# A state-space convolution and a gated MLP on one core: late groups rounded by ScalarE, seven absolute values on ScalarE, single PSUM banks for three stages, and another order

## The chip, the core and the metric

The kernel runs on one core of a Trainium2 chip. A core has five engines that run side by side, each through its own instructions in order: TensorE (PE, with its weight loads shown apart as PEld), VectorE (DVE), ScalarE (ACT), GpSimd (POOL) and SyncE (SP). SP, POOL and ACT also issue DMA transfers, each through its own queue. Products of TensorE land in PSUM, eight banks of 512 float32 values per partition; everything else is kept in SBUF, 128 partitions wide. The metric is the device time of one launch in microseconds.

## The reference

Two blocks on a sequence of 2048 rows and 576 channels, each behind a layer norm with a modulation that comes from a condition vector `c`:

```python
mod = (silu(c) @ w_mod).reshape(1, 6, 1, 576)         # sa, ca, ga, sb, cb, gb
h = layernorm(x) * (1 + ca) + sa
x = x + ga * A(h)                                      # state-space convolution
h = layernorm(x) * (1 + cb) + sb
x = x + gb * B(h)                                      # gated MLP

# A: K[d, l] = Re sum_n C[d,n] exp(dt[d] A[d,n] l) dt[d] B[d,n],  n < 128, l < 2048
#    y = causal convolution of h with K along l (by FFT) + h * Dskip
# B: z = gelu(x @ w_in); g = w_sp @ layernorm(z2) + b_sp; (z1 * g) @ w_out
```

What matters here is A. Its kernel K needs, for each channel and pole, an exponential of the real part and the sine and cosine of the imaginary part of `dt A l`.

## The kernel before, in words

The program has two parts. `ssm` does block A in the first quarter of the span; the class `Mlp` does block B in the rest. The change touches `ssm` only.

`ssm` computes the convolution by a hand-made transform of length 2048, split as 32 by 64. It is built of units, Python generators that issue a few instructions at each step. The units that matter:

- `O`, `P`: the poles. From the raw parameters, logarithms, phases and their three-part bf16 splits are computed on DVE and ACT and stored to DRAM (`pa_d`, `pb_d`, on POOL's queue); `Q` loads them back as `lb`, `lc`, `la` (POOL's queue), one set for nine groups.
- `M` (`mod_unit`): one of the six modulation vectors: a product over the partitions, a copy, a product with ones, and a last step that differs by vector. `M2`, `M1`, `M0` give what the first layer norm needs, `M0` in an alternation of ACT and DVE that splits its result in bf16 parts; `M3` to `M5` are for the MLP. `i` (POOL's queue) and `w` (SP's queue) load the weights.
- `S`, `R`, `A`: layer-norm statistics of four row blocks (`x` and `j` load them, two buffers), the rows themselves on DVE, and `ln_half`, the first transform: sixteen small products in two 288-column halves, four results of 288 columns each, copied by ACT to `st1o` and stored to `u1_d` in DRAM (POOL's queue).
- for each of 36 groups of 16 channels: `e` (an exponent product and two exponentials on ACT), `t` (a phase product, the rounding to the nearest turn, the absolute value, and two sines on ACT), `p` (products of these on DVE), `k` (64 small products into `kab`), `1` (`k1_unit`, the 32-point product, copied to the tile `k1`).
- `u`, `z`, `v`, `y`: for each of 36 slices the second transform of the rows (`u`, with a DMA that swaps real and imaginary halves, `uu` to `uu`), the product with the transformed kernel (`z`), the way back (`v`, stored to `v_d`), and the last transform with the residual (`y`, stored to `x1_d`). `U`, `W`, `X` load their inputs on SP's queue.

In `t_unit`, `ROUNDED` says how the phase is reduced to a fraction of a turn. For a group in the set (all 36 before), PE adds and takes away a large constant in PSUM: four products of 512 columns for the constant and eight of 256 for the phase, twelve in all, and the remainder is left in PSUM. DVE takes its absolute value by masking the sign bit into `ct`, ACT takes the sine of the remainder and the sine of the absolute value, shifted (a cosine). For a group outside the set, PE makes four products of 256 columns, ACT copies with the constant added, DVE subtracts both to get the remainder in SBUF, masks the sign bit there, and ACT takes both sines from SBUF.

PSUM is shared out in two pools: `ps2`, two buffers of two banks each, for `M`, `A`, the first product of `e`, `t` and `1`; and `ps1`, four buffers of one bank, for the second product of `e`, for `k`, `u`, `z`, `v`, `y`.

The sequence on every engine is written out by hand in the string `ORDER`: a word such as `t14` takes the next step of unit `t` for number 14, and each engine runs its instructions in just this order (`Pinned` keeps it). Capital letters without steps issue loads or change pools. `C0` closes the pools of the early units (`O`, `P`, `M`, `S`, `R`, `A`) and opens those of `u`, `z`, `v`, `y`; `D0` ends the tables' pools and starts the MLP's; the words `L0` to `L17` are the MLP's first loads and scalings. Line 182 in the profile is the helper that issues every pinned instruction, so groups are told apart by their tiles: `ps` and `pk` are the two PSUM pools, `et` exponentials, `ft` a group's phase and sines, `pg` the products of `p`, `kab` and `k` the results of `k` and `1`.

Of the kernel before, what the change touches and what calls it, by code (L numbers as in the profile page):

```python
# [12 lines left out]
I32 = mybir.dt.int32  # L13
# [16 lines left out]
ROUNDED = set(range(36))  # L30
COPIED = set()
ORDER = """
B2 i2 B0 B7 O0 O0 O0 O0 O0 O0 j1 O0 M2 O0 O0 i1 x0 O0 O0 O0 O0 B6 O0 B4 O0 M1 O0 O0 O0 B1 B3 O0 O0 S0 M2 O0 w3 O0 O0 O0 P0 O0 O0 B5 O0 O0 M2 P0 S1 S0 O0 g1 S0 P0 O0 P0 S1
S0 P0 P0 S0 Q0 P0 g0 P0 M2 S0 i0 e0 e0 t0 t0 M1 M1 M1 t2 P0 P0 t0 S1 e0 P0 t2 t2 P0 S1 t0 R0 P0 R2 M0 e2 M0 M0 e2 M0 e1 e5 e1 M0 e0 O0 R1 t1 e5 e4 M0 P0 t1 e1 t1 P0 t3 p0
p0 t1 P0 p0 M0 t3 t3 k0 M0 e3 t2 e5 e4 e1 M0 P0 k0 R3 10 P0 e3 e3 e2 10 S1 P0 A0 S1 A0 A0 A0 A1 e2 p2 P0 e3 A1 A1 A1 A0 A2 p1 r2 p1 p1 t3 p2 P0 A2 A1 P0 A2 k1 A2 A3 k1 A3
A3 R5 A3 p3 R4 t4 p2 r3 A2 t4 t4 11 11 e4 A4 R7 A3 P0 A4 k2 R6 A4 p3 j2 A4 A5 A5 O0 A5 A4 t4 P0 S2 A5 M3 k2 e4 M3 A6 S2 A6 A6 w4 A6 e6 P0 t5 e5 S2 e6 p4 S2 t5 M3 t5 M3 M4
a4 12 t5 S2 A5 M4 P0 M4 M3 p3 e6 p4 12 P0 P0 k3 M4 A7 A7 P0 e6 A7 A7 e8 P0 k3 O0 e7 e8 M4 t6 e7 13 A6 t6 O0 R9 w5 x3 R8 13 M5 t6 P0 M5 p4 t6 A8 S3 S3 A7 P0 A8 A8 A8 k4 S3
S3 A9 a5 Q1 A9 S3 A8 R10 A9 A9 r6 M5 R11 P0 k4 O0 R12 14 M5 e7 p6 14 p6 P0 O0 R13 P0 A10 A9 A10 e7 e8 p6 p5 O0 O0 A10 P0 A10 A11 p5 A11 A11 A11 r7 k6 A12 A10 p5 R14 A12
A12 k5 t7 A11 A12 t7 t7 A13 t7 P0 k5 k6 A13 R15 O0 A13 O0 p7 P0 t8 A13 t8 t8 15 p7 15 A12 t8 A14 p7 A14 A14 A14 A13 e8 P0 k7 p8 A15 A15 P0 k7 A14 A15 e10 A15 M5 e9 e10
A15 e9 C0 e11 e9 e10 p8 p8 e11 e9 t10 k8 t10 Q2 e11 t9 e10 U5 t10 t10 t9 p10 t9 U1 t11 U9 t11 t11 U2 U0 u1 u5 u1 t9 c2 16 16 17 p10 17 p10 u2 k8 U6 u5 t14 p9 u0 k10 t14  # L40
t11 u2 18 p9 t14 U10 z5 e14 k10 u5 18 e12 e11 u6 u1 p9 e14 z5 c0 u0 e12 e14 v5 110 u0 p11 e13 e12 p11 v5 k9 110 U7 p11 u6 e13 z1 e18 v5 c1 e15 e14 z1 U13 k11 e18 z0 t12
# [153 lines left out]
def ssm(tc, I, x1_d, consts_s, dram, mod_d, mlp):  # L195
# [3 lines left out]
    HC = 288  # L199
    CW = 16 * 9 * 128  # L200
    with ExitStack() as ctx:
# [1983 lines left out]
```

## Time and profile before

| what | value |
|---|---|
| median of 3 runs | 1782.7 us (1779.5 to 1788.4) |
| the profiled execution | 1781.2 us, span 1779.5 us |
| PE busy | 1665.9 us, 94% of the span |
| DVE busy | 1233.0 us, 69% |
| ACT busy | 828.9 us, 47% |
| POOL busy | 248.3 us, 14% |
| mean granted PE clock | 0.969 |
| table loads on ACT | 44, 1283 ns each |
| state-space part | from 0 to about 447 us |

Engine shares are averages over stages with different limits, so the stage is what must be looked at. Busy PE is not PE at its peak: the ends of matmuls are modelled, and a matmul that is pipelined behind another counts from its own start, so durations of neighbours overlap. A float32 product is issued as two instructions. What a unit of work costs an engine is therefore read from start to start, where the engine runs without a gap.

### The profile page before, as it was taken

Reading aid. Unit: us, or ns where it says so; the run is one execution under the profiler, and the core shown is the slowest. Engines: PE = TensorE matmul, PEld = TensorE weight load, DVE = VectorE, ACT = ScalarE, POOL = GpSimd, SP = SyncE. Lnnn points to the kernel's source line nnn. Section 1 sums busy time; section 2 is a strip of 40 time slices with the busy share of each in tenths; the row PEclk is TensorE's granted clock in tenths of the full one; section 3 lists DMA queues with packets and bytes.
Section 4 is the critical chain, followed back from the end, with each engine's and each line's share of the span. In section 5 each row is a group of like instructions: output and inputs, shape, how many; then the busy total and the mean of one; then the engine's idle time right before and its main releaser. Section 6 shows DMA issues by size and latency. Waiting matters only on the chain.

```text
span 1779.5 us, 38363 instructions
## 1 busy us (share of the span) xinstructions
PE 1665.9 (94%) x16246; PEld 1240.0 (70%) x16246; DVE 1233.0 (69%) x2173; ACT 828.9 (47%) x1117; POOL 248.3 (14%) x412
## 2 busy tenths in 40 slices
PE   2677899997899999999989999999999999999999
PEld 0334556565455545787878888888888888888887
DVE  5776787766999998788898768688344478344432
ACT  4867888863577666445434443234232223122210
POOL 3242232232222211000000000000111100111100
PEclk9577999999899999999999999999999999999999
DMA  8274667689688778777665886773766573556531
GB/s 245 63 241 155 182 185 209 175 217 276 202 273 275 242 226 278 285 250 245 224 210 174 298 291 224 270 245 124 245 223 229 196 234 99 193 196 218 193 111 41
DMA packets 182939, 376.42 MB, mean 212 GB/s; under 512 B 39104, under 2 KB 102976, under 8 KB 182000
## 3 DMA queue, kind: packets, MB, share of 16 engines
q1 hardware_dynamic: 138304, 168.56, 31.1%
q0 software_dynamic: 37984, 178.55, 30.4%
q10 hardware_dynamic: 6480, 26.86, 3.7%
q8 instruction: 127, 2.08, 0.5%
q14 instruction: 44, 0.36, 0.1%
HBM read 263.18 MB, written 101.31 MB: 205 GB/s over the span
## 4 chain that ended last, share of the span: by engine, by line
PE 67%; DVE 15%; DMA 5%; issue 4%; ACT 2%; POOL 1%; SPq 0%; ACTq 0%; DVEq 0%; POOLq 0%
PE ps L182 58%; PE pk L182 9%; DVE bsz L182 2%; DMA zset<-set_d 2%; DVE n L182 1%; DVE zset L182 1%; DVE rq L182 1%; DVE gt L182 1%; DVE wso L182 1%; DMA uu<-uu 1%; DVE wsp L182 1%; DVE nt L182 1%; DMA wsst<-in_w_spT 1%; DVE bsx L182 1%; DMA z_d<-z 1%
## 5 line engine op out<-in xcount | busy, mean ns | idle before, releaser
L182 PEld LDWEIGHTS <-zset 128*128 128x128 f16 x7182 | 701.3, 98 | 97.4 <-DVE zset L182 8.1
L182 PE MATMUL ps<-wsp,zset 128*128 128x256 f16 x6048 | 669.1, 273 | 9.9 <-DVE zset L182 6.3
L182 PE MATMUL pz<-wz,nt 128*128 128x512 f16 (+1 forms) x1120 | 223.6, 360 | 8.0 <-ACT nt L182 2.7
L182 ACT ACTIVATE z<-gt 128x1024 f16<-128x1024 f32 x56 | 59.0, 1054 | 282.0 <-DVE gt L182 281.9
L182 PEld LDWEIGHTS <-nt 128*128 128x128 f16 x1120 | 109.3, 99 | 116.3 <-issue 5.4
L1893 POOL DMA_DIRECT2D zset<-set_d x96 | 50.8, 529 | 872.9 <-PE ps L182 619.3
L182 DVE SCALAR_TENSOR_TENSOR gt<-ps,sc,bsp 128x512 f32<-128x512 f32 x36 | 27.0, 750 | 207.6 <-PE ps L182 205.9
L182 PE MATMUL ps<-wout,z 128*128 128x288 f16 x1344 | 170.1, 286 | 0.0
L182 PEld LDWEIGHTS <-z 128*128 128x128 f16 x1344 | 131.2, 98 | 33.3
L182 PE MATMUL ps<-n2o,zset 128*128 128x256 f16 x1134 | 128.2, 273 | 0.0
L182 DVE SCALAR_TENSOR_TENSOR gt<-ps,sc,gt 128x512 f32<-128x512 f32 (+1 forms) x180 | 122.2, 696 | 7.6
L182 DVE TENSOR_TENSOR raw<-raw 128x512 f32<-128x512 f32 (+2 forms) x228 | 119.1, 528 | 10.6 <-DMA raw<-z_d 6.3
L182 ACT ACTIVATE zset<-raw 128x1792 f16<-128x1792 f32 x48 | 81.2, 1692 | 61.4 <-PE ps L182 33.4
L182 DVE TENSOR_TENSOR zset<-raw,zset 128x1792 f16<-128x1792 f32 x48 | 97.0, 2020 | 17.2 <-ACT zset L182 17.2
L182 DVE TENSOR_TENSOR z<-ps,z 128x512 f32<-128x512 f32 (+1 forms) x126 | 71.9, 598 | 36.8 <-ACT z L182 26.7
L182 DVE TENSOR_TENSOR pg<-et,ft 128x1024 f32<-128x1024 f32 x72 | 85.9, 1218 | 11.9 <-ACT et L182 6.5
L182 DVE TENSOR_TENSOR zz<-pk,uu 128x1024 f32<-128x1024 f32 x36 | 43.9, 1222 | 39.0 <-PE pk L182 31.3
L182 PE MATMUL pk<-zz,small 128*128 128x512 f32 x144 | 69.4, 608 | 0.2 <-DVE zz L182 0.2
L182 ACT ACTIVATE wsp<-raw,sc 128x1792 f16<-128x1792 f32 x25 | 44.6, 1784 | 42.7 <-DVE raw L182 35.0
L182 ACT ACT_TABLE_LOAD x44 | 56.5, 1283 | 16.4 <-DMA et<-in_A_B_re 14.3
L182 DVE TENSOR_SCALAR ft<-ps 128x1024 int32<-128x1024 int32 x36 | 43.8, 1221 | 27.7 <-PE ps L182 26.8
L182 ACT ACTIVATE z<-z,sc 128x1024 f32<-128x1024 f32 x21 | 24.1, 1148 | 75.6 <-DVE z L182 71.9
(299 smaller groups left out, 2357.2 us busy)
## 6 DMA issues: line engine op xcount, KB each, us to landing
zset<-set_d POOLq DMA_DIRECT2D x96, 896.0 KB, 4.9
raw<-z_d SPq DMA_DIRECT2D x48, 512.0 KB, 5.5
set_d<-zset ACTq DMA_DIRECT2D x24, 896.0 KB, 6.0
z_d<-z POOLq DMA_DIRECT2D x32, 576.0 KB, 8.7
zset<-wa_d POOLq DMA_DIRECT2D x18, 896.0 KB, 4.9
raw<-in_w_spT SPq DMA_DIRECT2D x25, 512.0 KB, 4.5
set_d<-zset SPq DMA_DIRECT2D x12, 896.0 KB, 5.3
u_d<-st1o POOLq DMA_DIRECT2D x16, 576.0 KB, 4.6
```

What stands on the lines that cost most here:

```text
L182: return self.tc.keep_in_program_order(f(*a, **k))
L1893: self.nc.gpsimd.dma_start(o, self.set_d[f, j - 1] if j else self.wa_d[f])
```

## The change

Five things are changed, all in `ssm`:

1. Eleven groups (14, 16, 18, ... 34) leave `ROUNDED`, so ACT and DVE reduce their phase and PE makes four products instead of twelve.
2. For the rounded groups 0, 2, 4, ... 12 (`ON_ACT`) the absolute value is taken by an ACT instruction instead of DVE.
3. `mod_unit`, `ln_half` and `k1_unit` take single banks from `ps1` (two, four and two of them) instead of two-bank buffers from `ps2`; each copy out of PSUM is made per bank, so two where there was one. `ps2` is left to `t`, the first product of `e`, and two late uses in the MLP's start.
4. `z_unit` takes the tile `uu` of its slice after its products are issued, not before.
5. `ORDER` is another string. It has 1341 words instead of 1251: two more for each of the 16 `A` units, one more for each of the 36 `1` units, two more for each of the 11 groups of point 1.

```diff
-ROUNDED = set(range(36))
+ROUNDED = set(range(14)) | set(range(15, 36, 2))
 COPIED = set()
+ON_ACT = set(range(0, 14, 2))
...
         def mod_unit(k):
             wm = wmt.pop(k)
-            pm = ps2()
+            pm = [ps1(), ps1()]
             for hh in range(2):
                 for kt in range(6):
                     j = kt % 4
-                    T.matmul(pm[32 * j:32 * j + 32, hh, :HC], ec[:, kt:kt + 1].to_broadcast([96, 32]),
+                    T.matmul(pm[hh][32 * j:32 * j + 32, :HC], ec[:, kt:kt + 1].to_broadcast([96, 32]),
                              wm[hh][:, kt], start=kt < 4, stop=kt >= 2, skip_group_check=True)
             yield
             mpart = ep.tile([128, D], F32, name="mpart", bufs=1)
-            A.activation(v3(mpart), pm[:, :, :HC], AF.Copy)
+            for hh in range(2):
+                A.activation(v3(mpart)[:, hh], pm[hh][:, :HC], AF.Copy)
...
         def ln_half(k):
...
-            pms = [ps2(), ps2()]
+            pms = [ps1() for _ in range(4)]
...
-                        T.matmul(pms[g // 2][64 * t:64 * t + 64, g % 2, :HC], x[rows], y[rows, c], start=st, stop=not st, skip_group_check=True)
+                        T.matmul(pms[g][64 * t:64 * t + 64, :HC], x[rows], y[rows, c], start=st, stop=not st, skip_group_check=True)
                 yield
             o = ep.tile([128, 4, HC], F32, name="st1o")
-            for k, pm in enumerate(pms):
-                A.activation(o[:, 2 * k:2 * k + 2], pm[:, :, :HC], AF.Copy)
+            for g, pm in enumerate(pms):
+                A.activation(o[:, g], pm[:, :HC], AF.Copy)
                 yield
...
-                V.tensor_single_scalar(ct.bitcast(I32), pa.bitcast(I32), 0x7FFFFFFF, op=ALU.bitwise_and)
+                if g in ON_ACT:
+                    A.activation(ct, pa, AF.Abs)
+                else:
+                    V.tensor_single_scalar(ct.bitcast(I32), pa.bitcast(I32), 0x7FFFFFFF, op=ALU.bitwise_and)
                 yield
                 A.activation(f, pa, AF.Sin, scale=-TWO_PI)
...
         def k1_unit(g):
             c, gi = divmod(g, 8)
             kk = kab.pop(g)
-            pm = ps2()
+            pm = [ps1(), ps1()]
...
-            pk = pm[:, :, :256].rearrange("p h (c k) -> p k h c", c=8)
-            if g in COPIED:
-                V.tensor_copy(o, pk)
-            else:
-                A.activation(o, pk, AF.Copy)
+            for h in range(2):
+                pk = pm[h][:, :256].rearrange("p (c k) -> p k c", c=8)
+                if (g, h) in COPIED:
+                    V.tensor_copy(o[:, :, h], pk)
+                else:
+                    A.activation(o[:, :, h], pk, AF.Copy)
+                yield
...
         def z_unit(n):
             c, i = place(n)
-            uu = st.pop(n)
             w = CHW[c]
...
             yield
+            uu = st.pop(n)
             zz = st[n] = sb.tile([128, 2, 512], F32, name="zz")
```

The rest of the diff is the same edit in the last step of `mod_unit`, and the string `ORDER`. Marks of the order that the prediction uses, as word positions before and after: the first `M0` 90 and 85, the first `A0` 140 and 168, the last `A15` 385 and 474, `C0` 387 and 482, `Q2` 398 and 314, `D0` 1132 and 1210, the end 1251 and 1341.

More of the change, by code (lines that the diff above doesn't have):

```diff
@@ L60 @@
+L17 y15 y18 y17 W19 y15 y19 y19 y14 y19 y17 y18 L13
 """
@@ L426, in mod_unit @@
                 mrow = ep.tile([128, D], F32, name="gar", bufs=1)
-                if k == 4:
-                    A.activation(v3(mrow), src, AF.Identity, bias=one)
-                else:
-                    A.activation(v3(mrow), src, AF.Copy)
+                for hh in range(2):
+                    if k == 4:
+                        A.activation(v3(mrow)[:, hh], src[hh], AF.Identity, bias=one)
+                    else:
+                        A.activation(v3(mrow)[:, hh], src[hh], AF.Copy)
                 yield
@@ L604, in k1_unit @@
             kk = kab.pop(g)
-            pm = ps2()
+            pm = [ps1(), ps1()]
             for i in range(4):
```

72 lines of the change are left out of this document (38 added, 34 removed).

## The prediction

> **What bounds the kernel now.** I read first the busy time in stretches, cut where the state-space part changes character, then single rows of the timeline that date the cuts. Columns of the first view: stretch, its length, then busy microseconds (and instructions) of PE, PEld, DVE, ACT, POOL, the granted clock, DMA share, GB/s.
>
> ```profile
> 0.00:54.00 54.00, 18.63 (x87) 6.97 (x91) 31.64 (x94) 30.18 (x59) 16.72 (x32) 0.97 0.81 227
> 54.00:82.00 28.00, 18.27 (x178) 8.18 (x178) 20.85 (x35) 22.01 (x29) 7.48 (x12) 0.50 0.14 27
> 82.00:168.00 86.00, 62.62 (x1202) 33.33 (x1193) 60.55 (x132) 58.83 (x88) 28.80 (x44) 0.70 0.59 186
> 168.00:200.00 32.00, 25.35 (x438) 14.18 (x438) 19.79 (x21) 23.74 (x33) 9.58 (x17) 0.89 0.92 264
> 200.00:390.00 190.00, 184.81 (x3410) 113.51 (x3412) 149.99 (x155) 155.30 (x213) 52.87 (x95) 1.00 0.65 180
> 390.00:447.00 57.00, 46.96 (x412) 32.64 (x401) 32.08 (x80) 24.96 (x33) 17.61 (x28) 0.91 0.96 278
> 447.00:1779.00 1332.00, 1309.30 (x10548) 1031.22 (x10548) 918.11 (x1659) 513.87 (x665) 115.23 (x185) 1.00 0.65 217
> ```
>
> The cuts, from the timeline (start, duration, what):
>
> ```profile
> 53.63 4.06 PE L182 MATMUL ps<-k,ec 96*32 96x288 f32 x24
> 81.77 0.49 PE L182 MATMUL ps<-gsp,cs 32*64 32x288 bf16 x8
> 169.03 0.79 POOL L182 DMA_DIRECT2D u_d<-st1o  x1 [2.06 <-ACT st1o L182]
> 389.78 0.41 SPq L182 DMA_DIRECT2D mrow<-mod_d  x1
> ```
>
> In the order string these are the first `M0` (stretch B begins), the first `A0` (C), the store behind the last `A15` (D), and `D0`, which sets up the MLP (E). The MLP, 447 to 1779 us, is the same code after the change; PE is busy 1309 of its 1332 us and I leave it at its length. So everything is decided by when E ends. In D PE is busy 25.35 + 184.81 = 210 of 222 us: that stage is PE's. In B and C nothing is full: ACT 22 of 28 and 59 of 86 us, DVE 21 and 61, and PE runs at half to 0.7 clock. What PE waits for there:
>
> ```profile
> PE ps L182 <- ACT st1o L182: 9.9, 11, 1.6
> PE ps L182 <- ACT ft L182: 8.4, 6, 2.5
> ```
>
> Those 18.3 us are the two-bank `ps` buffers: `ln_half` needs both, and one is held by a `t_unit` or by the copy of the previous half.
>
> **The change part by part.** The prices on PE come from start to start in D at full clock:
>
> ```profile
> 198.03 0.24 PE L182 MATMUL pk<-dsk,small 128*32 128x4 f32 x8
> 199.13 1.16 PE L182 MATMUL pk<-k,cst 128*128 128x128 f32 x8
> 200.22 0.60 PE L182 MATMUL ps<-sel,lb 48*128 48x512 bf16 x4
> 202.94 0.39 PE L182 MATMUL ps<-sel 48*128 48x512 bf16 x2
> 203.16 0.27 PE L182 MATMUL ps<-sel,lc 48*128 48x256 bf16 x2
> 203.38 0.38 PE L182 MATMUL ps<-sel 48*128 48x512 bf16 x2
> 203.82 0.38 PE L182 MATMUL ps<-sel 48*128 48x512 bf16 x2
> 205.77 1.88 PE L182 MATMUL pk<-u,small 128*128 128x512 f32 x4
> 207.49 1.88 PE L182 MATMUL pk<-zz,small 128*128 128x512 f32 x4
> 209.30 0.69 PE L182 MATMUL ps<-small,kab 64*64 64x64 f32 x32
> ```
>
> A `k` costs 1.10 us (198.03 to 199.13), a `z` 1.09 (to 200.22), a rounded `t` 0.88 (202.94 to 203.82), one `u` 0.86 (two in 205.77 to 207.49), a `v`, two such products, 1.72, a `1` 0.69 (its duration), either product of an `e` 0.22 (a pair of 512 columns, 202.94 to 203.16). A group that isn't rounded on PE keeps two of the four 256-column pairs of its `t` (203.16 to 203.38): 0.22, so each of the 11 groups frees 0.66 us of PE.
>
> ACT and DVE, mean durations, and two rows that show neighbours overlapping:
>
> ```profile
> L182 ACT ACT_TABLE_LOAD x44 | 56.5, 1283 | 16.4 <-DMA et<-in_A_B_re 14.3 <-PEq L2174 0.7 <-DVE ft L182 0.4
> L182 ACT ACTIVATE ft<-ft,consts_s 128x1024 f32<-128x1024 f32 x36 | 40.9, 1150 | 0.3 <-issue 0.3
> L182 ACT ACTIVATE ft<-ps 128x1024 f32<-128x1024 f32 x36 | 36.6, 1024 | 27.0 <-DVE ft L182 26.8
> L182 ACT ACTIVATE k<-ps 128x512 f32<-128x512 f32 x36 | 21.4, 600 | 8.9 <-PE ps L182 8.8
> L182 ACT ACTIVATE st1o<-ps 128x576 f32<-128x576 f32 x32 | 19.1, 647 | 12.6 <-PE ps L182 5.7 <-DMA u_d<-st1o 3.2 <-issue 2.8
> L182 ACT ACTIVATE kab<-pk 128x256 f32<-128x256 f32 x36 | 13.9, 392 | 7.3 <-PE pk L182 7.3
> L182 DVE TENSOR_TENSOR pg<-et,ft 128x1024 f32<-128x1024 f32 x72 | 85.9, 1218 | 11.9 <-ACT et L182 6.5 <-PE pk L182 3.9 <-ACT ft L182 1.4
> L182 DVE TENSOR_SCALAR ft<-ps 128x1024 int32<-128x1024 int32 x36 | 43.8, 1221 | 27.7 <-PE ps L182 26.8
> L182 DVE TENSOR_SCALAR t_n_C_im<-t_ph 128x432 f32<-128x432 f32 x2 | 0.8, 388 | 0.1
> L182 DVE TENSOR_SCALAR et<-et 128x144 f32<-128x144 f32 x3 | 0.7, 232 | 0.1
> 206.85 2.35 DVE L182 TENSOR_TENSOR pg<-et,ft 128x1024 f32<-128x1024 f32 x2
> 207.89 1.08 ACT L182 ACTIVATE uu<-pk 128x512 f32<-128x512 f32 x2
> ```
>
> Two 602 ns copies take 1.08 us, two 1218 ns products 2.35: I take 0.11 off each ACT and 0.08 off each DVE instruction, not off the table loads.
> - Absolute value on ACT, 7 groups: DVE -1.14 us each. The row of before has no such ACT instruction; it reads what the sine with 1024 ns reads and writes as much, so 0.92. Whether it needs a table load is not shown: between none and two of 1283 ns each, 18 us for the seven. I take none, because copies and squares run between sines and exponentials in before without one.
> - Rounding on ACT, 11 groups: one more 0.92 on ACT and, the second sine input being SBUF now, up to 0.13 more (1150 against 1024). On DVE one more pass over 128x1024 from PSUM, 1.14 (as the 1218 ns row); the absolute value then reads SBUF: between 388 ns (432 columns) and the 1221 of PSUM; the rows of 144 and 432 columns extend to 0.71, less 0.08, which I take. DVE +0.63 a group.
> - Halves instead of pairs: the copy of a `1` was 600 ns, now two of 392 (the 256-column row): +0.07. `st1o` had two of 647, now four of 288 columns, between 392 and 647, 0.42 on the line between them, 0.31 in a row: +0.16 a unit.
> - Table loads: walking both strings and counting each change among exponential, logarithm, arctangent and sine gives 43 and the one for the gelu, the 44 of the row; for the new string 33 and 1. Ten fewer, 12.8 us of ACT: one each in A, B and C, seven in D.
> - The bank split lets `e` and `t` no longer stand in line with `ln_half` and `1`: of the 18.3 us of waits in B and C between none and all go. It gives PE more to overlap with, but no engine less to do. `z_unit` taking `uu` later only lets 8 instead of 4 `z` products be issued before the swap of their `u` is issued.
>
> On the tables the Trainium skill (ScalarE: Activation LUTs, "What ACT_TABLE_LOAD costs") gives a drain of about 1.38 us with each load, 2.66 us per switch, by which ten fewer would free an estimated 26.6 us. The next two rows disagree: the load begins 0.02 us after the copy before it ends and the sine 0.01 us behind the load, so 1.28 is the whole price.
>
> ```profile
> 203.21 0.42 ACT L182 ACTIVATE kab<-pk 128x256 f32<-128x256 f32 x1
> 203.65 1.28 ACT L182 ACT_TABLE_LOAD   x1
> 204.94 1.15 ACT L182 ACTIVATE ft<-ft,consts_s 128x1024 f32<-128x1024 f32 x1
> ```
>
> The Trainium skill (ScalarE: Activation LUTs, "Rules for kernel authors") advises VectorE, not ScalarE, for simple element-wise work, which speaks against this change; by 1024 against 1221 ns from PSUM the trace doesn't bear that out here. The Trainium skill (ScalarE: Activation LUTs, "Table sets: the hidden batching unit") has abs in every set; no run shows it yet.
>
> **The other order.** I counted every step between the same marks in both strings and priced it as above; for before the sums give ACT 18, 56, 174 us in B, C, D and PE 216 in D, against 22, 59, 179 and 210 measured, near enough for differences.
> - A (to the first `M0`): ACT -4.6, DVE -4.5. Its end is the weight load behind `i0`, one POOL slot earlier. Taken as 0.
> - B (to `A0`): ACT +9.8, DVE +10.7. `M3` and `M4` stand here now (mpart and mod copies, +2.6), one more `t` with two sines, one absolute value, four `pt` copies, two late exponentials, two statistics.
> - C (to the last `A15`): ACT +16.5 (nine sines +8.7, five absolute values +4.6, seven `e` for four +2.8, `st1o` +2.6, one rounding +0.9, `M3`, `M4` gone and one table load less -3.3), DVE +2.8. `Q2`, three loads and a fill on POOL, is moved ahead of the rows' last stores; POOL is busy 28.8 of 86 us there, and its tiles' last reader (`t6`) is issued earlier, so I add nothing; if it did wait, the `u1` stores stand behind it. `w4` moves ahead of `A0` and the `x3` load stays behind `A7`.
> - D: ACT -9.8, DVE -12.2, PE -21.9: 27 rounded `t` become 12 and 10 short ones (-11.0), eight `e` products, three `k`, two `u`, two `1`, a `z` and a `v` fewer (-1.8, -3.3, -1.7, -1.4, -1.1, -1.7).
> - E: PE +4.5 (a `z`, two `u`, a `v` come here).
>
> So five whole groups are pulled ahead of the LN rows' end, and D shrinks by that and by ten of the short `t`. B: 31.8 us of ACT work don't fit 28 us; at full ACT 32, at today's share (22 of 28) 40; I take 36, +8, a share of 88%. C: 75.3 us of ACT fit in 86, at today's share (59 of 86) it would be 110; with the two waits for `ps` mostly gone I take 90, +4, bounds -4 (four of the 18 us given back) and +24. D: at today's PE share (97% of the summed 216) 222 becomes 200, -22; if ACT, then 169 of it, keeps its 81% share, 209, -13; I take -20. E: 0 to +4.5, as PE is busy 47 of 57 there; +2. Sum 0 + 8 + 4 - 20 + 2 = -6, with ends at -22 and +28.
>
> **The rivals.**
> 1. The early stage absorbs it all. For it: nothing is full in B and C, and PE's clock of 0.50 to 0.70 shows idling; with `ps` free the added `t` fill holes. Against: ACT would run at 98% in B. B +4, C -4, D -22, E 0: -22 at best, -18 taken.
> 2. ACT becomes the bound in D: every unrounded `t` puts two more hand-overs between PE and the sines. Against: ACT's sum there falls. D -13, then 0 + 8 + 4 - 13 + 2 = +1.
> 3. Slower: the LN chain (`M0` to `A15`) is paced by hand-overs between engines in program order, not by ACT's sum; each added instruction ahead of an `st1o` copy then delays it in full, and B and C keep today's shares: +12 + 24 - 20 + 2 = +18. It decides once B and C together grow by more than 27 us, the last `A15` store then beginning after 196 us instead of 169. For it: ACT idles in C at 68% although rows wait.
> A fourth, that the absolute value does bring table loads (up to +18 on ACT in B and C), would end in the third.
>
> **How the numbers follow.** The profiled execution took 1781.2 us, its span 1779.5, the median of the three runs is 1782.7, 1.5 above it. Forecast: 1781.2 - 6 = 1775.2, as a median 1776.7, say 1777. Chances: forecast 0.45, rival 1 (1765) 0.25, rival 2 (1784) 0.15, rival 3 (1801) 0.15. Half a per cent, what a measurement tells from no change, is 8.9 us. A third of the forecast's own spread (1 to 13 us gained) lies beyond it: faster 0.15 + 0.25 = 0.40; same 0.30 + 0.14 = 0.44; slower 0.15 + 0.01 (the upper end of rival 2) = 0.16. The range leaves out the far ends of rivals 1 and 3: 1762 to 1794; the forecast's own is 1770 to 1782.
>
> **What would show it.** Table loads 34; the three `ft` passes at 0.92 to 1.0 (ACT), 1.2 and about 0.7 us (DVE); no PE wait for `st1o` above 3 us in sum; first `A0` near 90 us, the last `A15` store near 181, `D0` near 382, the MLP's first product 6 us earlier. I am wrong if the last `A15` store comes before 172 or after 196, or if PE's share in D falls under 92%.

## The result, and the profile after

The changed kernel took 1761.7 us (median; 1756.6 to 1764.0), the kernel before 1781.8 us on the same chip: a ratio of 0.9877, 95% interval 0.9841 to 0.9914 (the ratio is taken over the single runs and isn't the quotient of the two medians). Run a second time, word for word, it took 1758.9 us, ratio 0.9880 (0.9866 to 0.9895). So it is 20 to 22 us faster, where 6 were forecast. The measured time lies 0.3 us below the forecast's range and beside rival 1 (1765). One execution of a_both, a run told below, had a granted clock of 0.324 and took 5850.7 us; it is left out of that run's ratio.

The stretches of the changed kernel, cut at the same marks as the prediction's first view and with the same columns (busy time of PE, PEld, DVE, ACT, POOL, then granted clock, DMA share, GB/s):

```profile
0.00:50.00 50.00, 17.16 (x110) 7.26 (x110) 28.05 (x89) 27.41 (x60) 17.00 (x32) 0.86 0.90 248
50.00:78.00 28.00, 19.81 (x378) 11.56 (x378) 25.43 (x41) 26.96 (x46) 7.93 (x13) 0.88 0.32 70
78.00:169.00 91.00, 67.60 (x1177) 35.38 (x1179) 68.29 (x144) 77.08 (x145) 32.53 (x50) 0.68 0.55 170
169.00:372.00 203.00, 189.98 (x3550) 119.79 (x3545) 159.09 (x169) 166.12 (x258) 57.28 (x102) 0.98 0.71 202
372.00:436.00 64.00, 52.65 (x429) 35.06 (x419) 36.25 (x85) 25.48 (x35) 22.00 (x35) 0.88 0.93 274
436.00:1762.00 1326.00, 1307.77 (x10543) 1031.40 (x10541) 914.35 (x1654) 512.17 (x662) 112.47 (x181) 1.00 0.65 217
```

The timeline rows that date the cuts (start, duration, what), the last being the first product of the MLP:

```profile
50.24 2.13 PE L185 MATMUL pk<-k,ec 96*32 96x288 f32 x24 [0.43 <-DVE cga L185]
78.14 0.42 PE L185 MATMUL pk<-gsp,cs 32*64 32x288 bf16 x2
169.36 0.75 POOL L185 DMA_DIRECT2D u_d<-st1o  x1 [2.29 <-ACT st1o L185]
372.33 0.33 SPq L185 DMA_DIRECT2D mrow<-mod_d  x1
435.80 4.42 PE L185 MATMUL pz<-wz,nt 128*128 128x512 f16 x14 [0.69 <-ACT nt L185]
```

| stretch | before | after | moved | forecast |
|---|---|---|---|---|
| A, to the first `M0` | 53.6 | 50.2 | -3.4 | 0 |
| B, to the first `A0` | 28.1 | 27.9 | -0.2 | +8 |
| C, to the last `A15` store | 87.3 | 91.2 | +3.9 | +4 |
| D, to `D0` | 220.8 | 203.0 | -17.8 | -20 |
| E, to the MLP's first product (450.5 us before) | 60.7 | 63.5 | +2.8 | +2 |
| the rest of the span | 1329.0 | 1326.3 | -2.7 | 0 |

The last `A15` store starts 0.3 us later than before, though ACT is busy 26.96 + 77.08 = 104.0 us between the first `M0` and that store, against 22.0 + 58.8 in the prediction's rows of before, some 82 with the last microsecond. From the first `M0` to that store it is 119.1 us, and 115.9 in the second run, against 115.4 before: 22 us more of ACT cost 0 to 4 us. Marks of one program move by some microseconds between executions: in the profile of its second run the four later marks are 77.6, 165.5, 369.2 and 430.7 us, so that C is 87.9 and E 61.5 us there, while D is 203.8. I read nothing from differences below 5 us in a single mark.

Where ACT's early time came from is seen in the waits of its own queue, 50 to 170 us. First the kernel before (engine, tile, whom it waited for, sum, times, longest):

```profile
ACT ft L182 <- DVE ft L182: 12.2, 7, 4.1
ACT st1o L182 <- PE ps L182: 5.7, 5, 2.3
ACT st1o L182 <- DMA u_d<-st1o: 3.2, 1, 3.2
ACT st1o L182 <- issue: 2.8, 2, 1.7
```

The same view of the changed kernel:

```profile
ACT kab L185 <- PE pk L185: 5.4, 5, 1.5
ACT pt L185 <- DMA pa_d<-pt: 3.4, 1, 3.4
ACT ft L185 <- DVE ft L185: 3.1, 3, 1.4
```

ACT no longer stands before an `st1o` copy (11.7 us in three rows before, none now), and of the 12.2 us for which its sines waited for DVE's absolute value 3.1 are left. The work that the new order pulls ahead stands in these gaps. PE's own waits did not go away (50 to 168 us of the changed kernel; before, the first and the third were 9.9 and 8.4):

```profile
PE pk L185 <- ACT st1o L185: 10.7, 8, 3.9
PE ps L185 <- ACT et L185: 8.2, 5, 2.7
PE ps L185 <- ACT ft L185: 8.2, 4, 3.3
```

The prices, in the view that groups instructions (count, busy, mean ns):

```profile
L185 ACT ACT_TABLE_LOAD x34 | 43.6, 1283 | 9.1 <-DVE ft L185 5.7 <-DVE sc L185 2.2 <-PEq L2187 0.7
L185 ACT ACTIVATE ft<-ps 128x1024 f32<-128x1024 f32 x43 | 44.2, 1038 | 6.4 <-DVE ft L185 4.4 <-PE ps L185 1.4 <-ACT et L185 0.5
L185 ACT ACTIVATE st1o<-pk 128x288 f32<-128x288 f32 x64 | 22.4, 438 | 0.2
L185 DVE SCALAR_TENSOR_TENSOR ft<-ft,ps 128x1024 f32<-128x1024 f32 x11 | 13.4, 1216 | 1.8 <-ACT ft L185 1.7
L185 DVE TENSOR_SCALAR ft<-ft 128x1024 int32<-128x1024 int32 x11 | 7.7, 701 | 0.2
```

The 43 `ft<-ps` of ACT are 25 sines, 7 absolute values and 11 rounding copies. Loads, absolute values and every pass cost what the prediction said, or nearly so.

### The profile page after: what moved, and what is told of

Same layout as the page of the kernel before. It is cut to its first block, busy times and chain, and to the rows that moved or that the text cites. A ratio compares the mean times of both kernels' runs of the same rounds, so it can differ in the third digit from the quotient of the medians.

```text
span 1762.1 us, 38307 instructions
## 1 busy us (share of the span) xinstructions
PE 1655.0 (94%) x16158; PEld 1240.5 (70%) x16158; DVE 1231.5 (70%) x2179; ACT 835.2 (47%) x1203; POOL 249.2 (14%) x412
## 5 line engine op out<-in xcount | busy, mean ns | idle before, releaser
L185 DVE TENSOR_TENSOR raw<-raw 128x512 f32<-128x512 f32 (+2 forms) x228 | 119.2, 528 | 12.5 <-DMA raw<-z_d 8.2
L185 DVE TENSOR_TENSOR zset<-raw,zset 128x1792 f16<-128x1792 f32 x48 | 96.9, 2020 | 14.6 <-ACT zset L185 14.5
L185 ACT ACTIVATE z<-pz,sc 128x512 f32<-128x512 f32 (+1 forms) x96 | 52.3, 581 | 14.6 <-PE pz L185 8.6
L185 DVE TENSOR_TENSOR zz<-pk,uu 128x1024 f32<-128x1024 f32 x36 | 43.9, 1222 | 20.4 <-PE pk L185 17.1
L185 PE MATMUL ps<-n2q,wf 128*128 128x512 f16 x252 | 55.7, 379 | 0.0
```

The costliest lines, as they stand in the source:

```text
L185: return self.tc.keep_in_program_order(f(*a, **k))
```

## The experiments

All runs were timed in five rounds beside the kernel before, whose median stood between 1780.9 and 1783.2 us; "changed kernel" below means the two measurements above. The marks are from one profile each.

**The parts of the change.**

a_long: the changed kernel with the 11 groups rounded by PE again; DVE copies the remainder to SBUF, so that DVE keeps its place in the order and ACT loses the copy.

```diff
-            if g in ROUNDED:
+            if g in ROUNDED or g in SPARE:          # SPARE: the 11 groups
...
+                if g in SPARE:
+                    V.tensor_copy(f, pa)
+                    yield
+                    yield
+                    A.activation(f, f, AF.Sin, scale=-TWO_PI)
```

> The changed kernel with its own order, but with the 11 late groups rounded on PE again (twelve phase products instead of four); for them DVE takes the absolute value and copies the remainder to SBUF, in the steps where ACT copied and DVE subtracted. Same quantities computed. PE gets 11 x 0.66 = 7.3 us more, 10 of the 11 between the last A15 store and D0; ACT gets about 10 us less, DVE 5.5 us more. PE theory (that stretch, D, is PE's and the gain in it is PE relief): D0 6 us later than in the changed kernel (378 against 372), time 1768. Order theory (the new string alone carries the gain, the short phase products nothing): D0 within 1.5 us, time within 2 of 1762. ACT theory (ACT paces D): D0 earlier, time 1757 or less. The last A15 store stays at 169 +-1 by all three.

Measured: 1766.1 us, ratio 0.9909 (0.9890 to 0.9928); D took 199.2 us in its profile against 203.0 and 203.8, in an execution that was its fastest (1760.2). By the medians rounding by ACT is worth 4 to 7 us in the new order, by the intervals 0 to 11, and the profile does not show them in D.

a_dve: the changed kernel with the seven absolute values on DVE.

```diff
-ON_ACT = set(range(0, 14, 2))
+ON_ACT = set()
```

> The changed kernel with the seven absolute values back on DVE, nothing else. B and C get 7 x 0.92 = 6.4 us less on ACT and 8 us more on DVE. If ACT fills B (27 of 28 us busy) and C (76 of 90): first A0 and last A15 store earlier, by 1 to 5 us, time 1757 to 1761. If the early stage is paced by DVE or by hand-overs: last A15 store later by 2 to 8 us, time 1764 to 1770. If the early stage has room on both: within 1.5 us of 169, time within 2 of 1762.

Measured: 1763.1 us, ratio 0.9886 (0.9869 to 0.9902). No difference.

b_abs: the kernel before with these seven absolute values on ACT, in the old order.

```diff
+ON_ACT = set(range(0, 14, 2))
...
-                V.tensor_single_scalar(ct.bitcast(I32), pa.bitcast(I32), 0x7FFFFFFF, op=ALU.bitwise_and)
+                if g in ON_ACT:
+                    A.activation(ct, pa, AF.Abs)
+                else:
+                    V.tensor_single_scalar(ct.bitcast(I32), pa.bitcast(I32), 0x7FFFFFFF, op=ALU.bitwise_and)
```

> The kernel before with the seven absolute values on ACT, nothing else. ACT in B and C gets 6.4 us more, DVE 8 us less. Rival 3 of the prediction (the LN chain is paced by hand-overs, each added ACT instruction ahead of it delays it in full): last A15 store 4 to 6 us later (173 to 175 against 169), time 1786. Rival 1 (the early stage has room): within 1.5 us of 169, time within 2 of 1782. If DVE paces the early stage: last A15 store 2 to 6 us earlier.

Measured: 1782.1 us, ratio 0.9995 (0.9982 to 1.0009). No difference either; ACT's 7 us were hidden in the old order too.

b_short: the kernel before with the 11 groups rounded by ACT and DVE. The old order has four steps for a `t`, so copy, subtraction and absolute value are issued in one.

```diff
-ROUNDED = set(range(36))
+ROUNDED = set(range(14)) | set(range(15, 36, 2))
...
                 A.activation(f, pa, AF.Copy, bias=MAGIC)
-                yield
                 V.scalar_tensor_tensor(f, f, MAGIC, pa, op0=ALU.subtract, op1=ALU.subtract)
-                yield
                 V.tensor_single_scalar(ct.bitcast(I32), f.bitcast(I32), 0x7FFFFFFF, op=ALU.bitwise_and)
```

> The kernel before with its old order, two-bank buffers and all absolute values on DVE; only the 11 late groups are taken off PE rounding (ACT copy, DVE subtraction and DVE absolute value stand in the one step where the absolute value stood). PE 7.3 us less, ACT 10 us more, DVE 7 us more, nearly all after the last A15 store. PE theory: D0 5 to 7 us earlier than before (383 to 385 against 390), time 1775 to 1777. Order theory: no change, 1780 to 1783. ACT theory: D0 later, by up to 8 us, time up to 1790.

Measured: 1797.0 us, ratio 1.0073 (1.0056 to 1.0090). That is 14 us more than the kernel before, and D took 242.9 us, 22 us more, with fewer products on PE. The waits of D in it (168 to 411 us):

```profile
ACT ft L182 <- DVE ft L182: 21.2, 17, 3.4
DVE ft L182 <- ACT ft L182: 19.3, 9, 5.3
```

The first of them in the kernel before (169 to 390 us), and then in the changed one (169 to 372 us):

```profile
ACT ft L182 <- DVE ft L182: 14.5, 11, 2.9
```

```profile
ACT ft L185 <- DVE ft L185: 1.3, 1, 1.3
```

So rival 2's mechanism is real: a copy, a subtraction and a mask in a row make ACT and DVE wait for each other when no other work stands between them. The steps that the new order puts there take these waits away; they give little beyond that.

a_order: the changed kernel with parts 1 and 2 undone (a_long and a_dve together). What is left is the order, the single banks and the later `uu`.

```diff
-ON_ACT = set(range(0, 14, 2))
+ON_ACT = set()
...
-            if g in ROUNDED:
+            if g in ROUNDED or g in SPARE:          # and the rest of a_long
```

> The changed kernel's order and single banks alone: the 11 late groups rounded on PE (DVE takes the absolute value and copies the remainder to SBUF), the seven absolute values on DVE. If order and banks carry most of the gain: 1764 to 1768, of the 20 us three quarters or more. If the moved work carries it: 1774 or more. Undoing only the rounding had given 1766, undoing only the absolute values 1763.

Measured: 1766.5 us, ratio 0.9905 (0.9887 to 0.9923). Some 16 of the 20 to 22 us are the order's and the banks'. Between these two nothing decides: neither the new order with two-bank buffers nor the old order with single banks was run, so their shares stay open. In a_order's profile D is 201.1 us, and the time that is lost stands in E (69.6 us against 63.5 and 61.5); why isn't known.

**What the order gains by.** a_block: the changed kernel, but 51 words of `e`, `t`, `p`, `k` for the groups from 9 on that stand ahead of `C0` are moved behind it, in a block after `U3`.

```diff
-... p7 15 15 Q2 t11 P0 k4 R11 t11 p8 ... A15 15 P0 C0 16 U0 ... U3 16 p11 ...
+... p7 15 15 Q2 P0 k4 R11 p8 ... A15 15 P0 C0 16 U0 ... U3 t11 t11 e10 ... 16 p11 ...
```

> The changed kernel, with the 51 words of e, t, p and k for groups 9 and up that stand ahead of C0 moved in one block behind U3, otherwise the same string and the same work. About 9.5 us of PE, 18 us of ACT and 13 us of DVE work leave the stages before the last A15 store and come behind it. Room theory (the gain is whole groups computed in idle time of the early stage, which PE then lacks to do in D): last A15 store earlier by at most 8 us, D0 later by 5 to 15, time 1768 to 1776. Theory that the early stage was lengthened by these groups as much as D is shortened (the forecast's +12 and rival 3): last A15 store earlier by 10 or more, time within 3 of 1762 or below.

Measured: 1781.3 us, ratio 1.0003 (0.9985 to 1.0021): the whole gain is gone. The `A15` store comes 9.9 us earlier than in the changed kernel (6.0 earlier than in its second run), D takes 232.3 us. Its windows up to the store, and two of ACT's waits there (50 to 160 us):

```profile
50.00:78.00 28.00, 19.94 (x380) 11.44 (x373) 25.42 (x41) 26.86 (x48) 7.95 (x13) 0.88 0.30 65
78.00:160.00 82.00, 55.67 (x1123) 30.16 (x1124) 56.16 (x130) 55.31 (x121) 33.01 (x51) 0.76 0.61 190
ACT st1o L183 <- PE pk L183: 6.5, 5, 1.6
ACT st1o L183 <- DMA u_d<-st1o: 3.9, 2, 2.2
```

Beside the changed kernel's two rows, ACT has 21.9 us less, DVE 12.1 and PE 11.8, and the stage is 9 us shorter; with the moved work gone, ACT waits before its `st1o` copies again (10.4 us). In D the same work costs 29 us. That difference, some 20 us (22 by the second run's marks), is what the change is worth. Since the block is also badly placed, 29 is an upper bound for the cost of this work in D.

**How full ACT is in the early stage.** b_act and a_act put 24 words of eight 16-column copies into the old and the new order, between the first `M0` and the last `A15`.

```diff
+        def heat(n):
+            for i in range(8):
+                A.activation(hot, small[:, 0, :16], AF.Copy)
```

> The kernel before with 24 words that each copy 16 columns eight times on ACT (0.9 us a word), eight between the first M0 and the first A0, sixteen from there to the last A15; their output is not used. ACT gets about 7 us more in B and 14 us more in C, near the 26 us that the change put there. Room theory (holes of the early stage take it, in the old order as well): first A0 later by at most 2 us, last A15 store by at most 5, time up to 1787. Hand-over theory (rival 3): last A15 store 12 to 21 us later, time 1794 to 1803. If the room comes from the new string or the single banks only: in between, 6 to 12 us.

> The changed kernel with 192 copies of 16 columns on ScalarE between the first M0 and the last A15 (8 words of 8 before the first A0, 16 words of 8 behind it); in the kernel before, the same words took 215 ns a copy, 41.3 us in all, and moved the last A15 store by 27.8 us and the end by 25 to 28 us. If ScalarE alone paces the early stage of the changed kernel (27.0 of 28 us busy before A0, 76.1 of 90 us behind it), nearly all of the 41 us shows: A15 store near 200 to 208 us, time near 1792 to 1802. If the new order gave ScalarE more room than the old one had, A15 stays under 190 us and the time under 1780. If what is pulled ahead simply waits behind these copies, the time ends at about that of the kernel before with the copies, 1805 to 1812.

Measured: b_act 1809.3 us, ratio 1.0141 (1.0117 to 1.0164); a_act 1797.1 us, ratio 1.0098 (1.0084 to 1.0113). The added copies in a_act:

```profile
L184 ACT ACTIVATE hot<-small 128x16 f32<-128x16 f32 x192 | 41.8, 218 | 6.3 <-ACT k L184 1.0
```

In the old order 41.3 us of them moved the `A15` store by 27.8 us (169.0 to 196.8) and the time by 26. In the new one 41.8 us moved it by 31.8 to 35.7 (to 201.2, from the two profiles of the changed kernel) and the time by 35 to 38. So even the old order, with ACT idle for three tenths of B and C, took in only some 13 us of evenly spread ACT work. Rival 3's premise holds in part, and the new order's 22 us cost 0 to 4 us because of where they stand: in the `st1o` and `ft` gaps shown above. Nor did the new order make room for more; there is less left than before. By itself a_act looks as its first theory has it, an early stage that ACT alone paces; the next run speaks against that.

a_early: the changed kernel with the exponentials of the groups 0 to 13 replaced by copies.

```diff
-            A.activation(e[:, 1024:], pb, AF.Exp)
+            A.activation(e[:, 1024:], pb, AF.Copy if g < 14 else AF.Exp)     # both exponentials of e
```

> The changed kernel with the exponentials of the groups 0 to 13 replaced by copies (left out: the exponential itself), so that some 7 or 8 table loads less stand before C0, 9 to 10 us of ScalarE, with the same program otherwise. If ScalarE alone sets the pace of the early stage, the last A15 store comes 7 to 10 us earlier than in the changed kernel (165.5 and 169.4 us in its two profiles), so at 156 to 161, and the time is 1749 to 1754. If the early stage is a balance like stage D, A15 moves by at most 3 us and the time stays at 1757 to 1761.

Measured: 1762.1 us, ratio 0.9887 (0.9866 to 0.9908): nothing gained. Six table loads were saved, not seven or eight. C, and ACT's longest wait in 50 to 170 us:

```profile
78.00:168.00 90.00, 64.38 (x1145) 34.03 (x1141) 67.79 (x142) 68.50 (x134) 32.60 (x50) 0.71 0.54 166
ACT ft L185 <- DVE ft L185: 10.2, 3, 4.1
```

ACT did 68.50 instead of about 76 us of work in C and waited the rest for DVE (10.2 us instead of 3.1); the `A15` store stayed at 169.8. ACT alone is not the bound of this stage: adding to it costs three quarters and more of what is added (a_act), taking from it alone gives nothing.

**What bounds D.** a_tabs: the changed kernel with eight pairs of a one-column exponential and sine in D, so 48 table loads instead of 34.

```diff
+        def toggle(n):
+            A.activation(tiny[:, 0:1], one, AF.Exp)
+            A.activation(tiny[:, 1:2], one, AF.Sin)
```

> The changed kernel with eight pairs of one-column activations (an exponential and a sine) spread between C0 and D0, which put about 16 more table loads there, 20 us of ACT time; the pairs' outputs are not used. PE theory (D is PE's, the seven loads saved there are worth nothing): time 1762 to 1766. ACT theory (the saved loads are part of the gain): D0 later by 8 to 20 us, time 1770 to 1782.

Measured: 1776.1 us, ratio 0.9957 (0.9940 to 0.9974), D 220.3 us:

```profile
167.00:387.00 220.00, 193.09 (x3539) 120.23 (x3532) 159.84 (x169) 186.06 (x287) 56.91 (x102) 0.97 0.67 186
```

Some 21 us of ACT (14 loads of 1283 ns, 16 small operations of 203) cost 14 to 17 us. PE is busy 193 of 220 us: in D it waits 15.2 us for ACT here, in the changed kernel 4.4. So ACT time added at eight places reaches PE. By this price the loads that the change saves would be part of its gain; no run put just those back.

a_cop: the changed kernel with one of the two `k` copies of groups 14 to 35 on DVE.

```diff
-COPIED = set()
+COPIED = {(g, 1) for g in range(14, 36)}
```

> The changed kernel with one of the two copies of the product k of the groups 14 to 35 (22 of 72, 390 ns each on ScalarE, 8.6 us) on VectorE instead. If ScalarE's time in stage D counts, as the 16 added table loads there say (14 us for some 21 us), it ends 4 to 6 us earlier: 1756 to 1759, D0 4 to 6 us earlier than in the run of the same program beside it. If VectorE counts as much (133.9 of 172 us busy against ScalarE's 137.1), it stays within 2 us; if VectorE counts more there, it ends up to 9 us later, 1764 to 1771.

Measured: 1759.5 us, ratio 0.9880 (0.9864 to 0.9895). No difference: 8.6 us less of ACT and as many copies more on DVE balance, or neither counts.

a_all: the changed kernel with the other 11 late groups rounded by ACT and DVE too, in the four steps they have.

```diff
-ROUNDED = set(range(14)) | set(range(15, 36, 2))
+ROUNDED = set(range(14))
```

> The changed kernel with the other 11 groups of 14 to 35 rounded by a copy on ScalarE and a subtraction on VectorE too: per group a copy of about 1.06 us more on ScalarE and a subtraction of 1.22 us more on VectorE, and 16 rounding products less on TensorE (3.4 us a group). If TensorE bounds stage D, the 11 groups save up to 37 us of it and the time falls by some 15 to 20 us as the forecast had it for the first 11: 1742 to 1748. If ScalarE and VectorE count there as the added table loads say, the 11 copies (11.7 us) and 11 subtractions (13.4 us) cost as much as is saved: within 5 us of the changed kernel, or slower by up to 10 us.

Measured: 1766.5 us, ratio 0.9928 (0.9913 to 0.9942): 5 to 8 us slower than the changed kernel, as its second theory said. Its reason isn't shown: these groups have no steps between copy, subtraction and mask, and the wait of b_short is back (170 to 377 us),

```profile
DVE ft L185 <- ACT ft L185: 17.3, 10, 3.3
```

where the changed kernel has 0.8 us of it in D. The 37 us that this expectation gave PE are wrong (3.4 us a group is no price of these products; see a_pe).

Four runs take work from one engine or several in D, with the program otherwise the same. a_noexp: exponentials of the groups 14 to 35 replaced by copies. a_pe: no rounding products for the odd groups from 15 on. a_novec: one of DVE's four last products left out for the groups from 14 on. a_both is a_noexp with a_pe, a_three all three.

```diff
-            A.activation(e[:, 1024:], pb, AF.Exp)
+            A.activation(e[:, 1024:], pb, AF.Copy if g >= 14 else AF.Exp)    # a_noexp, both exponentials
...
-                magics(2112, True)
-                phases((768, 0), False, False)
-                magics(2240, False)
-                phases((1536, 1792), False, True)
+                if g < 14:                                                   # a_pe
+                    magics(2112, True)
+                phases((768, 0), g >= 14, g >= 14)
+                if g < 14:
+                    magics(2240, False)
+                    phases((1536, 1792), False, True)
...
-            V.tensor_tensor(pi[:, :, 1], s3, pi[:, :, 1], op=ALU.mult)
+            if g < 14:                                                       # a_novec
+                V.tensor_tensor(pi[:, :, 1], s3, pi[:, :, 1], op=ALU.mult)
```

> The changed kernel with the exponentials of the groups 14 to 35 replaced by copies of the same shape (left out: the exponential itself, so their magnitudes are wrong), so that ScalarE's tables need not be changed there: some 16 table loads of 1283 ns less, about 20 us of ScalarE. If ScalarE's time sets the length of stage D, the end comes 14 to 20 us earlier: 1739 to 1746. If the stage is bound by TensorE (190 of 203 us busy), it gains at most 4 us. If the three engines hold each other up, about half: 1748 to 1752.

> The changed kernel without the rounding products of the 11 odd groups 15 to 35 (left out: the reduction of the phase to one turn; nothing takes its place on ScalarE or VectorE): per group 4 products of 48x512 at 379 ns and 4 of 48x256 at 270 ns less, 2.6 us, 28.6 us in all. If TensorE bounds stage D, the end comes 20 to 29 us earlier: 1731 to 1740. If ScalarE does, at most 4 us: 1756 or later. If they hold each other up, about half: 1745 to 1750.

> The changed kernel without the last product of VectorE in each of the groups 14 to 35 (left out: one of the four parts of the pole factors isn't multiplied by the sine): 22 operations of 687 ns, 15.1 us of VectorE less, nothing else changed. If VectorE's time sets the length of stage D, 10 to 15 us earlier: 1745 to 1750. If ScalarE or TensorE does, within 3 us of the changed kernel. If the three hold each other up, 4 to 7 us earlier.

> Both of the first two at once: exponentials replaced by copies for the groups 14 to 35, and no rounding products for the odd ones of them (left out: the exponential and the reduction of the phase there); ScalarE some 20 us less, TensorE 28.6 us less. If one engine bounds stage D alone, this gains no more than the relief of that engine by itself (by at most 4 us). If TensorE and ScalarE hold each other up, more than the sum of the two: 25 to 35 us earlier, 1725 to 1735. If VectorE (159 of 203 us busy) then takes over, less than that: 1735 to 1742.

> The three reliefs of stage D at once (left out: the exponential, the reduction of the phase and one of the four parts of the pole factors, in the groups 14 to 35 and the odd ones of them): 14 table loads and 18 us of ScalarE, some 14 us of TensorE by its busy time, 15 us of VectorE less. From the last A15 store to D0 the changed kernel takes 203 to 204 us, with two reliefs 192.5. If the engines hold each other up, the third adds at least as much as alone (4 us) and D takes 180 to 188 us, the time 1740 to 1748. If the transfers set a floor (0.73 busy with two reliefs), D stays at 190 to 193 us and the time at 1750 to 1755.

| kernel | taken away in D | time | ratio, 95% interval | D |
|---|---|---|---|---|
| changed, second run | nothing | 1758.9 | 0.9880 (0.9866 to 0.9895) | 203.8 |
| a_noexp | ACT 18 us (14 table loads) | 1757.0 | 0.9856 (0.9842 to 0.9871) | 200.9 |
| a_pe | PE 6 to 7 us | 1757.8 | 0.9851 (0.9831 to 0.9872) | 199.7 |
| a_novec | DVE 15 us | 1760.0 | 0.9872 (0.9853 to 0.9891) | 199.0 |
| a_both | ACT 18, PE 6 to 7 | 1752.8 | 0.9835 (0.9811 to 0.9858) | 192.5 |
| a_three | all three | 1751.6 | 0.9828 (0.9802 to 0.9854) | 194.0 |

What a_pe takes off PE I had put at 28.6 us, from mean durations. The row of these products in D, of the changed kernel:

```profile
L185 PE MATMUL ps<-sel 48*128 48x512 bf16 x48 | 9.2, 379 | 0.0
```

and of a_pe:

```profile
L185 PE MATMUL ps<-sel 48*128 48x512 bf16 x4 | 0.8, 382 | 0.0
```

48 products of 379 ns stand for 9.2 us of busy time, 192 ns each, since each overlaps the next. With the 256-column products (9.2 to 6.2 us and 9.2 to 6.1) a_pe frees 14.5 us by the busy time of these groups; by the prediction's start-to-start price it is 11 x 0.66 = 7.3. All of PE together is busy 184.2 us of D in a_pe and 189.9 in the changed kernel, 5.7 less, and D is 3.3 to 4.1 us shorter. So this run could not have given the 20 to 29 us of its first theory, and it does not exclude that D is PE's.

D of a_three and of a_noexp:

```profile
169.00:363.00 194.00, 181.34 (x3461) 113.77 (x3452) 146.27 (x147) 147.65 (x243) 57.76 (x102) 0.99 0.73 206
```

```profile
168.00:369.00 201.00, 186.55 (x3553) 117.42 (x3543) 158.84 (x169) 148.30 (x243) 57.69 (x102) 0.99 0.72 204
```

Each relief alone gives up to 5 us of D, ACT's and PE's together 11, all three 10: far from the 40 us of work that a_three leaves out. By time only a_both and a_three lie clear of the interval of the changed kernel's second run. Of the expectations of the single reliefs, a_noexp's time speaks for PE as the one bound, a_pe's for ACT, and a_novec's against DVE; a_both's time lies between its ranges. a_three's time is that of its second expectation, a floor; D lies 1 us above it. What the floor is can be read in the waits of its D (169 to 363 us):

```profile
DVE zz L185 <- PE pk L185: 19.8, 13, 7.9
DVE pg L185 <- PE pk L185: 14.1, 8, 5.7
ACT uu L185 <- PE pk L185: 11.8, 11, 4.6
PE pk L185 <- DMA u<-u_d: 4.2, 1, 4.2
```

In all, ACT and DVE wait 72 us for PE there, and PE and DVE 6.8 us for transfers. Of D's 194.0 us PE is idle for 12.7; in the changed kernel it is 13.0 of 203.0, in a_both 12.5 of 192.5. So what is left of D goes with PE's busy time, and the transfers, whose engines are busy 0.73 of this D and 0.93 of the changed kernel's E, are hardly waited for. That is a reading of waits and not a test: the fixed order, in which an engine that is done sooner waits for the same partners, isn't told apart from PE.

a_again is the changed kernel itself.

> The changed kernel once more, word for word, to see how far its own marks move between two profiles and to sharpen its ratio. Both theories: the ratio stands between 0.984 and 0.991, within the interval of the first time. In the first profile the last A15 store started at 169.4 us, D0 at 372.3 us and the first product of the MLP at 435.8 us; profiles of kernels with nearly the same program had 164.5 to 166.0, 363.7 to 368.7 and 428.6 to 432.3. If these marks move by up to 5 us here too, differences of that size between kernels say nothing.

Measured: as told at the top; the marks moved by up to 5 us.

No version was measurably faster than the changed kernel while computing the whole: a_cop and a_dve equal it within the intervals.

## Why the prediction was wrong

- The failed steps are "Taken as 0" for A and "I take 36, +8, a share of 88%" for B. Together they measured -3.6 where +8 was forecast. Between the two profiles the span fell by 17.4 us, 11.4 more than forecast: A and B make 11.6 of it and the MLP, which I left at its length, 2.7, while C, D and E together fell 2.9 us less than forecast. B holds 26.96 us of ACT work in 28: 96%, not 88%. "31.8 us of ACT work don't fit 28 us" was also a sum 3 us too large: by the windows A and B together hold 27.4 + 27.0 = 54.4 us of ACT instead of 30.2 + 22.0 = 52.2, so +2 and not -4.6 + 9.8 = +5. This isn't one profile's chance: in 15 profiles of the new order (all but a_act's, with its added copies) the first `A0` begins at 76.0 to 81.8 us, where "near 90" was forecast.
- In A the wait was wrong as well. "Its end is the weight load behind `i0`" isn't what PE waits for. In the kernel before it is `cga`, a product of VectorE:

```profile
51.27 0.61 PE L182 MATMUL ps<-sel 48*128 48x512 bf16 x2 [3.25 <-DVE cga L182]
```

  From there 2.4 us of products of a `t` and an `e` run without a gap up to the first `M0` (53.63). After the change these stand ahead of the wait, and `cga` releases PE 1.0 us earlier, at 50.24 (the first of the rows that date the cuts). Together that is A's 3.4 us.
- C, "+4", came out in the first profile (91.2 against 87.3, with ACT at 85%), not in the second (87.9), and both lie within the bounds of -4 and +24. That the number was met is luck. Its reason, "with the two waits for `ps` mostly gone", does not hold: PE waits 10.7 us for `st1o` now and 16.4 for `et` and `ft`, where it was to be under 3 for the first. What went away are ACT's waits, for PE's `st1o` products and for DVE's absolute value.
- Rival 1, "the early stage absorbs it all", came true in the stage that it names (-3.6 for A and B, +3.9 for C; it had +4 and -4). Its reason, "nothing is full in B and C", is only half right: b_act shows that evenly spread ACT work isn't absorbed there. The place of the work decides.
- Rival 3's decision point, an `A15` store after 196 us, wasn't reached (169.4), although with the copies of b_act it was (196.8): its mechanism exists in part (27.8 us for 41.3 us added, not "in full"), and the change doesn't set it off.
- D, "I take -20", measured -17.8, and PE's share of it hardly moved: PE is busy 209.3 of 220.8 us before and 189.9 of 203.0 after, 19.3 less where 21.9 was forecast. But the split is another. Of the 21.9 us, 6.6 were to come from ten `t` being short (10 x 0.66; the rest of the -11.0 is five whole `t` pulled ahead) and 15.3 from the work pulled ahead. D before, and in a_long, which has the pulled-ahead work without the short `t`:

```profile
169.03:389.78 220.75, 209.29 (x3828) 127.28 (x3829) 168.74 (x175) 178.01 (x244) 62.45 (x112) 0.98 0.68 192
164.50:363.74 199.24, 192.10 (x3597) 119.90 (x3599) 163.68 (x169) 157.13 (x248) 56.66 (x103) 1.00 0.71 202
```

  The pulled-ahead work took 17 us off PE, the short `t` two more, and D is no shorter with them (a_order: PE 192.7 of 201.1 us). In the old order they even cost 22 us of D (b_short).
- "In D PE is busy 210 of 222 us: that stage is PE's" holds in one direction only. ACT time added there costs 14 to 17 of 21 us, because PE then waits for ACT. With work taken off, ACT and DVE wait for PE, and D less PE's busy time stays at 10.5 to 15.5 us in all five relief runs (13.0 in the changed kernel). So the sum over PE gave nearly the right number, for a reason that the waits bear out and no run tests by itself.
- Of the two marks that were to show me wrong, the `A15` store came before 172 us (169.4, 165.5), and PE's share of D stayed above 92% (189.98 of 203, 94%); that share says little, as a_tabs has it at 88% with PE work unchanged.
- E, +2 (measured +2.8, and +0.8 in the second profile), 34 table loads, no loads for the absolute value and the prices of DVE's passes held. ACT's copies and absolute values, in the row of 1038 ns, lie just above the 0.92 to 1.0 us named.
- On the Trainium skill's advice to give simple element-wise work to VectorE (ScalarE: Activation LUTs, "Rules for kernel authors"): a_dve and b_abs show no difference either way, and the 1038 ns of ACT against 1222 of DVE stand after as before.

## What to carry to other kernels

In a program whose engines run a fixed order, an engine's idle time is not free room: the same 41 us cost 28 when spread evenly, while 22 us in the right gaps cost at most 4. So look at what the engine that gets the work waits for, row by row, and ask whether the new work stands in those gaps. A stage in which several engines are 80 to 95% busy is not the fullest one's alone: here work added to the second one, ACT, cost two thirds of its length and more, since PE then waited for it, work taken from ACT or DVE gave little, since they then waited for PE, and what shortened the stage was moving whole units, with their share of every engine, to a stage with gaps. The price of pipelined products is taken from start to start, never from mean durations.

## What the runs showed of the hardware

PE's rate in the middle of the early stage is either full or half, and which one it is changes where the marks fall. The first `M0` product, 24 instructions, takes 2.13 us in the changed kernel's row above and 4.06 in the prediction's row of before. In a_cop, the same program up to there, it took the longer time again:

```profile
52.39 4.05 PE L185 MATMUL pk<-k,ec 96*32 96x288 f32 x24
```

All profiles with the old order have 3.85 to 4.06 us; there PE waits 0.9 to 3.8 us for `cga` (DVE) a few microseconds ahead of it, and a pair of its 512-column products is followed by the next after 0.42 us instead of 0.22. With the new order PE has no wait above 1 us between 42 and 49 us, and in all profiles but that one the rate has doubled by the first `M0`, at 45 to 51 us. The Trainium skill (TensorE: Matmul & The Clock Gate, "The HAM clock gate") has the clock at half until PE has been busy for a window of about 3.4 us, a window that runs freely, so that the moment differs between runs. That the moment differs, the traces show; the length they don't bear out. In a_cop PE has no wait above 0.3 us from 41.7 to 61 us and still runs its 256-column products at half rate at the end of it, 19 us later (0.42 us a pair; 0.27 at full rate):

```profile
60.60 0.42 PE L185 MATMUL ps<-sel,la 48*128 48x256 bf16 x2
```

A ends where this product begins, so its 1.9 us count in B. What the rate costs at the end isn't known, since no run sets it by itself: in a_cop's profile `A0`, the `A15` store and `D0` come 4.2, 3.6 and 4.3 us later than in the second run of the changed kernel and the span is 2.8 us longer, but a_cop also differs in D, and its median is within 1 us of the changed kernel's.
